# Sorted block attention and a residual MLP on one core: SyncE in program order, mixing of batches 2 and 3 moved to ScalarE one stage earlier, score and product groups in pairs

## The chip, the core and the metric

The kernel runs on one NeuronCore of one Trainium2 chip. The metric is the device time of one execution in microseconds (us), measured on that core. The engines are named as in the profile: PE is TensorE (matmuls; PEld is its weight load), DVE is VectorE, ACT is ScalarE, POOL is GpSimd and SP is SyncE, which here issues DMAs only. All engines run their own instruction streams and meet through semaphores.

## The reference

Four batches, eight heads, 768 rows, head dimension 64. A small matrix per head (8 x 8) is normalised five times by rows and columns. Keys and values are mixed block by block with it (blocks of 96 rows), attention runs inside each block, and the result goes through a residual MLP: a product over tokens, then two channel products with a ReLU between.

```python
k_sorted = np.einsum('bhij,bhjcd->bhicd', P, k_b)      # mixing of 8 blocks of 96 rows
v_sorted = np.einsum('bhij,bhjcd->bhicd', P, v_b)
scores = scale * q_b @ k_sb.transpose(...)             # inside a block
attn = softmax(scores);  x = attn @ v_sb               # -> (B, S, 512)
tok = np.einsum('ts,bsd->btd', w_tok, alpha1 * x + beta1)
u = x + lam * tok
ch = np.maximum((alpha2 * u + beta2) @ w_ch1, 0.0) @ w_ch2   # 512 -> 2048 -> 512
out = u + lam * ch
```

## The kernel before

Work is written out by hand in one global order. After an opening that handles batch 0's attention, a main loop goes over eight steps: batch `b` (0 to 3) by half `hf` (0 and 1, 384 rows each). This text calls a step (b, hf). Each step has two parts:

- "h 0" to "h 15": one unit of the first channel product each (`h_unit`: four matmuls of 128x384 on PE, then a ReLU on ACT from `h_ps` to `hTa` or `hTb`);
- "c 0" to "c 11": a quarter of one of three row tiles of the second channel product each (`ch_unit`: four matmuls of 128x512). After c 3, c 7 and c 11 a tile is complete: DVE multiplies it by lambda (`ost`), POOL adds `u`, SP stores it (two DMAs).

All other work is hung into this raster with `put(b, hf, kind, n, ...)` and runs right after unit `n` of that step. PE therefore executes channel matmuls with attention pieces of the next batch in between:

- `mix_v(b, n)` and `mix_k(b, n)` (n = 0 to 2) mix values and keys of batch b on PE into `mix_ps` and `kmix_ps`. An engine given as an argument copies the result out: `mix_v` one copy of 128x1024 into `mixed`, `mix_k` four copies of 64x512 into `kT`. `mix_matrix(b)` builds the small matrices for it (one matmul, six short DVE operations).
- `bounce_v(b)` writes `mixed` to DRAM (`vscr`), `back_v(b)` reads it back as `Vs` with tokens on partitions, in runs of 128 bytes.
- `load_kv(b)` loads `raw` (values, then keys) with POOL's DMAs, `load_q(b)` loads `qn` likewise (six DMAs); `q_cross(b, kt)` turns `qn` into `qT` with six transposing DMAs on SP. Batch 1 alone turns its queries on PE.
- `score(b, g, hf)` is eight matmuls into `sc_ps` and an exponential on ACT (`et`); `pv(b, g, hf)` is eight matmuls with `Vs` into `x_ps`, then on DVE a reciprocal and a multiplication (`x`), and, one call later, two operations for `a` (kept in the list `late`, run by `flush`).
- `tails` copies row remainders of `a` and `x`; `moe_tok` is six matmuls of the token product (`tok_ps`), two DVE operations (`toktmp`, `u16`) and a POOL add; `moe_cross` turns `u16` into `uT` with three transposing DMAs on SP; `moe_affine` makes `a2T` on DVE, the input of the h units.

Two PSUM pools serve this: `psA` has two slots (`sc_ps`, `x_ps`, `mix_ps`, `kmix_ps`, `repv_ps`), `psB` has four (`h_ps`, `ch_ps`, `tok_ps`). Slots go round, so a matmul group waits until the reader of the tile that held its slot is done.

The order on PE, DVE, ACT and POOL is the written one: the wrapper class `Engine` calls `tc.keep_in_program_order`. SP is used without the wrapper before the change, so the scheduling layer places its DMAs. Before, for batch b = 2 and 3, mixing lies in step (b-1, 0) from h 8 on, `q_cross` at h 11 there (but the scheduler places the six transposes of batch 2 on SP ahead of the first store of step (0, 1)), scores and products from c 8 of step (b-1, 0) to h 11 of step (b-1, 1), and the loads for batch b+1 at c 11 of step (b-1, 0).

Of the kernel before, what the change touches and what calls it, by code (L numbers as in the profile page):

```python
# [16 lines left out]
def kernel(  # L17
# [20 lines left out]
    nc = tc.nc  # L38

    B, H, S, D = q.shape  # L40
    NB = sort_net.shape[-1]
    BLK = S // NB
    C = H * D
    HID = moe_w_ch1.shape[1]
    NT = S // 128
# [4 lines left out]
    H4 = H // 2  # L50
# [23 lines left out]
    dve = Engine(nc.vector)  # L74
    act = Engine(nc.scalar)
    pool = Engine(nc.gpsimd)

    dram = ctx.enter_context(tc.tile_pool(name="dram", bufs=1, space=bass.MemoryType.DRAM))
    wts = ctx.enter_context(tc.tile_pool(name="wts", bufs=1))
# [380 lines left out]
    def pv(b, g, hf):  # L460
        if g == 0 and hf == 0:
            x_of[b] = moep.tile([128, 8, C], F16, name="x128", tag="x128", bufs=2)
            a1_of[b] = moep.tile([128, 8, C], F16, name="a1", tag="a1", bufs=1)
        ps = psa([128, 2, 512], FT, "x_ps")[:].rearrange("p a (k d) -> p a k d", d=128)
        et = ets[(b, g, hf)][:].rearrange("p a i t -> p (a i t)")
        for ii in range(4):
            for h2 in range(2):
                lo = (4 * h2 + ii) * BLK
                w = min(128, 8 * BLK - lo)
                pe.matmul(  # L470
                    ps[0:w, h2, ii, 0:D + 1], et[0:BLK, lo:lo + w],
                    Vs[b % 2][0:BLK, (2 * g + h2) * NB + 4 * hf + ii, 0:D + 1], start=True, stop=True,
                )
        rc = att.tile([128, 2, 4], FT, name="rcb", tag="rc", bufs=3)
        dve.reciprocal(rc[0:BLK], ps[0:BLK, :, :, D])
        dve.tensor_tensor(
            x_of[b][0:BLK, 4 * hf:4 * hf + 4, g * 128:(g + 1) * 128].rearrange("p k (a d) -> p k a d", a=2),
            ps[0:BLK, :, :, 0:D].rearrange("p a k d -> p k a d"),
            rc[0:BLK].rearrange("p a k -> p k a").unsqueeze(3).to_broadcast([BLK, 4, 2, D]), ALU.mult,
        )  # L480
        flush()
        late.append(lambda: first_affine(b, slice(0, BLK), slice(4 * hf, 4 * hf + 4), slice(g * 128, (g + 1) * 128)))

    late = []

    def flush():
        while late:
            late.pop()()

    def tails(x, lo, hi, eng):  # L490
        flush()
# [3 lines left out]
    def q_cross(b, kt):  # L495
        if kt == 0:
            qT_of[b] = att.tile([128, H4, S], F16, name="qT", tag="qT", bufs=1)
        nc.sync.dma_start_transpose(
            qT_of[b][:, :, kt * 128:(kt + 1) * 128], qn_of[b][:, kt, :, :].rearrange("p h d -> p (h d)"),
        )  # L500

    def q_turn_late(b, g, eng):
        if g == 0:
            qT_of[b] = att.tile([128, H4, S], F16, name="qT", tag="qT", bufs=1)
        ps = psb([128, S], F16, "qt_ps")
        for kt in range(NT):
            pe.transpose(
                ps[:, kt * 128:(kt + 1) * 128],
                qn_of[b][:, kt, 2 * g:2 * g + 2, :].rearrange("p a d -> p (a d)"), ident16[:],
            )  # L510
        eng(qT_of[b][:, g, :], ps[:])
# [37 lines left out]

    def bounce_v(b):  # L550
        for th in range(2):
            nc.sync.dma_start(
                vscr[b, :, th * HB:(th + 1) * HB, :], mixed[b][th * 64:(th + 1) * 64, :, :],
            )

    def back_v(b):
        nc.sync.dma_start(Vs[b % 2][0:BLK, :, 0:D], vscr[b].rearrange("x t d -> t x d"))

    w_tokT = const([128, NT, S], F16, "w_tokT")
    wp_of = {}  # L560
# [106 lines left out]
    def moe_cross(b, hf):  # L667
        uT = uT_of[(b, hf)] = att.tile([128, CT, 384], F16, name="uT", tag="uT", bufs=2)
        for m in range(3):
            nc.sync.dma_start_transpose(  # L670
                uT[:, :, m * 128:(m + 1) * 128], u16_of[b][:, 3 * hf + m, :],
            )

    def moe_affine(b, hf):
        for ci in range(CT):
            affine(b, hf, ci, uT_of[(b, hf)][:, ci, :], dve)
# [25 lines left out]
    def last_out(hT, cps, kk, kt):  # L702
        for n in range(2):
            c = slice(n * C // 2, (n + 1) * C // 2)
            if n:
                cps = psb([128, C // 2], FT, "ch_ps")
                for m in range(HT):
                    pe.matmul(
                        cps[:], hT[m][:, kk * 128:(kk + 1) * 128], W2p[:, m, c],
                        start=(m == 0), stop=(m == HT - 1),  # L710
                    )
            ost = att.tile([128, C // 2], FT, name="ost", tag="ost", bufs=2)
            dve.tensor_tensor(ost[:], cps[:, 0:C // 2], lamB[:, c], ALU.mult)
            dve.tensor_tensor(ost[:], ost[:], u_of[B - 1][kt][:, c], ALU.add)
            nc.sync.dma_start(out[B - 1, kt * 96:(kt + 1) * 96, c], ost[0:96, :])
            nc.scalar.dma_start(out[B - 1, TAIL + kt * 32:TAIL + (kt + 1) * 32, c], ost[96:128, :])

    def ch_unit(b, hf, kk, part=(0, HT)):
# [19 lines left out]
        act_out(out[b, TAIL + kt * 32:TAIL + (kt + 1) * 32, :], ost[96:128, :])  # L738

    ch_of = {}  # L740
    act_out = nc.sync.dma_start

    copy = dve.tensor_copy

# [72 lines left out]
    def put(b, hf, kind, n, *todo):  # L817
        at.setdefault((b, hf, kind, n), []).extend(todo)
# [6 lines left out]
        put(0, 0, "h", 4 + kt, lambda kt=kt: moe_tok(0, kt, psb))  # L825
    for ks in range(NT):
        put(0, 0, "h", ks, lambda ks=ks: prep_wtok(ks, 1, psb, (dve.tensor_copy, act.copy)[ks % 2]))
    for n in range(1, B):
        put(max(n - 2, 0), n > 1, *(("h", 10), ("c", 9))[n > 1], lambda n=n: mix_matrix(n))
    put(0, 0, "h", 9, lambda: moe_cross(0, 1))  # L830
    for g in range(CT):
        put(0, 0, "h", g, lambda g=g: first_affine(0, slice(0, 128), slice(0, NT), slice(g * 128, (g + 1) * 128)))
    for m in range(3):
        put(0, 0, "h", 10 + m, lambda m=m: first_back(m, psb))
    put(0, 0, "c", 3, lambda: moe_affine(0, 1))
    for b in range(1, B):
        p = b - 1
        off = 3 if b == 1 else 0
        for n in range(3):
            put(p, 0, "h", (13 if b == 1 else 8) + n, lambda b=b, n=n: mix_v(b, n, dve.tensor_copy))  # L840
        put(p, 0, "h", 15 if b == 1 else 10, lambda b=b: bounce_v(b))
        put(p, 0, "c", 4 if b == 1 else 0, lambda b=b: back_v(b))
        for n in range(3):
            put(
                p, 0, *(("c", 3 + 3 * n) if b == 1 else (("h", 15), ("c", 1), ("c", 4))[n]),
                lambda b=b, n=n: mix_k(b, n, ((act.copy, dve.tensor_copy)[(n + (b > 1)) % 2],) * 4),
            )
        for kt in range(NT if b > 1 else 0):
            put(p, 0, "h", 11, lambda b=b, kt=kt: q_cross(b, kt))
        for g in range(0 if b > 1 else H4):  # L850
            put(p, 0, "c", off + (1, 4, 7, 7)[g], lambda b=b, g=g: q_turn_late(b, g, (dve.tensor_copy, act.copy, dve.tensor_copy, act.copy)[g]))
        if b + 1 < B:
            put(p, 0, "c", 11, lambda b=b: load_kv(b + 1), lambda b=b: load_q(b + 1))
        seq = [("s", 0), ("s", 1), ("s", 2), ("p", 0), ("s", 3), ("p", 1), ("p", 2), ("s", 4), ("p", 3), ("s", 5),
               ("p", 4), ("s", 6), ("p", 5), ("s", 7), ("p", 6), ("p", 7)]
        if b == 1:
            when = [("h", 0), ("h", 1), ("h", 2), ("h", 3), ("h", 4), ("h", 5), ("h", 6), ("h", 7), ("h", 8), ("h", 9),
                    ("h", 10), ("h", 11), ("h", 12), ("h", 13), ("h", 14), ("h", 15)]
        else:
            when = [("c", 8), ("c", 9), ("c", 10), ("c", 10), ("c", 11), ("c", 11), ("h", 0), ("h", 1), ("h", 2), ("h", 3),  # L860
                    ("h", 4), ("h", 5), ("h", 6), ("h", 8), ("h", 9), ("h", 11)]
        for (kind, n), (ph, at_) in zip(seq, when):
            f = (lambda b=b, n=n: score(b, n // 2, n % 2, psa)) if kind == "s" else (lambda b=b, n=n: pv(b, n // 2, n % 2))
            put(p, 1 if ph == "h" else 0, ph, at_, f)
        last = [("h", 12), ("h", 15)][b == 1]
        put(
            p, 1, *last, lambda b=b: tails(a1_of[b], 0, C, dve.tensor_copy),
            lambda b=b: tails(x_of[b], 0, C, dve.tensor_copy),
        )
        put(p, 1, "h", 4, lambda b=b: moe_start(b))  # L870
        for kt in range(3):
            put(p, 1, "c", 4 if b == 1 else 3, lambda b=b, kt=kt: moe_tok(b, kt, psb))
        put(p, 1, "c", 4 if b == 1 else 3, lambda b=b: moe_cross(b, 0))
        put(p, 1, "c", 8 if b == 1 else 7, lambda b=b: moe_affine(b, 0))
        for kt in range(3):
            put(b, 0, "h", 2 * kt, lambda b=b, kt=kt: moe_tok(b, 3 + kt, psb))
        put(b, 0, "h", 4, lambda b=b: moe_cross(b, 1))
        put(b, 0, "h", 13, lambda b=b: moe_affine(b, 1))

# [50 lines left out]
```

## Time and profile before

| what | value |
|---|---|
| time, median of 3 runs | 275.54 us (274.01 to 275.88) |
| time of the profiled execution | 275.76 us |
| span of the profiled execution, first to last instruction | 274.0 us |
| mean granted PE clock | 0.994 |
| PE busy | 260.2 us (95% of the span) |
| DVE, ACT, POOL busy | 169.7, 117.1, 96.4 us |
| DMA moved | 31.04 MB, POOL's queue 40.1% and SP's queue 30.9% of 16 engines' span |

The profile gives the busy time of each engine, groups of equal instructions with their mean duration, waits with what ended them, a timeline, and DMAs with the time from issue to landing. In rows such as `raw<-in_v_dram` the tile written stands left of the arrow. Nearly all rows carry the line L65, because the wrapper records every operation; one goes by tile names. L498, L552, L557, L670 and L737 are SP's own lines before the change (`q_cross`, `bounce_v`, `back_v`, `moe_cross`, the store). The steps of the main loop begin on PE at about 39.6 (0,0), 72.6 (0,1), 103.2 (1,0), 132.9 (1,1), 163.9 (2,0), 195.3 (2,1), 223.8 (3,0) and 248.4 us (3,1).

### The profile page before, as it was taken

The numbers are of one execution on the slowest core, as the hardware profiler recorded it, in microseconds if no ns is written. First come the engines' busy times: TensorE is split into PE (matmuls) and PEld (weight loads), VectorE is DVE, ScalarE is ACT, GpSimd is POOL, SyncE is SP. The second block draws the span as 40 slices with busy tenths as digits, with TensorE's granted clock in tenths as the row PEclk, the third lists the DMA queues.
The fourth block names the chain that finished last, engine by engine and source line by source line (L and its number), as shares of the span: only waits on it lengthen the run. The fifth ranks groups of instructions, "written<-read, shape, count | busy, mean of one in ns | idle before, by whom it ended". The sixth has DMA issues, their size and how long they took to land.

```text
span 274.0 us, 5366 instructions
## 1 busy us (share of the span) xinstructions
PE 260.2 (95%) x2159; PEld 140.4 (51%) x2173; DVE 169.7 (62%) x351; ACT 117.1 (43%) x219; POOL 96.4 (35%) x104
## 2 busy tenths in 40 slices
PE   7998899999999999999999969999999999999993
PEld 3466555455556444554455424564465445545552
DVE  5787527896468978576778725586689755121032
ACT  2588547234787002553674002554674004604600
POOL 8647102701472094403560824402200746122000
PEclk9999999999999999999999997999999999999999
DMA  6999999998989942249399952149300223012012
GB/s 103 211 206 193 206 207 214 173 115 178 128 176 175 133 116 78 59 115 145 86 182 165 113 138 61 38 118 117 106 10 2 76 58 77 22 38 77 0 41 77
DMA packets 67372, 31.04 MB, mean 113 GB/s; under 512 B 56642, under 2 KB 63058, under 8 KB 67348
## 3 DMA queue, kind: packets, MB, share of 16 engines
q0 software_dynamic: 26352, 15.34, 40.1%
q1 hardware_dynamic: 40900, 15.30, 30.9%
q8 instruction: 17, 0.28, 0.4%
q14 instruction: 7, 0.06, 0.1%
q10 hardware_dynamic: 96, 0.07, 0.1%
HBM read 32.79 MB, written 8.65 MB: 151 GB/s over the span
## 4 chain that ended last, share of the span: by engine, by line
PE 77%; DVE 9%; DMA 6%; issue 3%; SPq 2%; ACT 2%; POOL 0%; DVEq 0%; POOLq 0%
PE h_ps L65 30%; PE ch_ps L65 21%; PE tok_ps L65 10%; PE x_ps L65 3%; DMA out_dram<-ost 2%; PE sc_ps L65 2%; DVE ost L65 2%; DVE a L65 2%; DVE x L65 2%; PE warm_ps L65 2%; DMA q<-in_q_dram 2%; DMA uT<-u 2%; PE mix_ps L65 1%; PE kmix_ps L65 1%; SPq L737 1%
## 5 line engine op out<-in xcount | busy, mean ns | idle before, releaser
L65 PE MATMUL h_ps<-a2T,W1p 128*128 128x384 bf16 x512 | 97.2, 328 | 2.4 <-DVE a2T L65 2.1
L65 ACT ACTIVATE hTa<-h_ps 128x384 bf16<-128x384 f32 x96 | 47.0, 492 | 95.3 <-PE h_ps L65 95.1
L65 PE MATMUL ch_ps<-W2p,hTa 128*128 128x512 bf16 (+1 forms) x287 | 67.3, 370 | 0.6
L65 POOL TENSOR_TENSOR ost<-ost,u 128x512 f32<-128x512 f32 x21 | 26.6, 1267 | 116.1 <-DVE ost L65 110.0
L65 PEld LDWEIGHTS <-W1p 128*128 128x128 bf16 x512 | 47.6, 99 | 35.3 <-issue 5.0
L65 PEld LDWEIGHTS <-hTa 128*128 128x128 bf16 x300 | 28.4, 98 | 29.0
L65 DVE TENSOR_TENSOR ost<-ch_ps,lamB 128x512 f32<-128x512 f32 (+1 forms) x25 | 16.7, 670 | 37.9 <-PE ch_ps L65 34.6
L65 POOL TENSOR_TENSOR u<-toktmp,x 128x512 f32<-128x512 f32 x18 | 29.2, 1635 | 6.7 <-DVE toktmp L65 6.6
L65 PE MATMUL tok_ps<-a,w_tokT 128*128 128x512 f16 x126 | 30.5, 386 | 0.0
L65 ACT ACTIVATE et<-sc_ps 96x768 f16<-96x768 f32 (+1 forms) x32 | 25.6, 812 | 10.8 <-PE sc_ps L65 10.8
L65 PE MATMUL ch_ps<-W2p,hTb 128*128 128x512 bf16 (+1 forms) x99 | 24.8, 370 | 0.1
L65 DVE TENSOR_TENSOR toktmp<-tok_ps,lamB 128x512 f32<-128x512 f32 x21 | 14.4, 687 | 11.8 <-PE tok_ps L65 10.5
L65 PEld LDWEIGHTS <-w_tokT 128*128 128x128 f16 x126 | 12.3, 99 | 14.5 <-issue 1.1
L65 DVE TENSOR_TENSOR u<-toktmp,x 128x512 f16<-128x512 f32 (+1 forms) x24 | 18.9, 800 | 0.7
L65 ACT ACTIVATE hTb<-h_ps 128x384 bf16<-128x384 f32 x32 | 15.7, 490 | 8.0 <-PE h_ps L65 7.6
L65 POOL DMA_DIRECT2D qn<-in_q_dram x18 | 16.0, 924 | 4.7 <-DMA raw<-in_v_dram 4.7
L65 DVE CAST kT<-kmix_ps 64x512 f16<-64x512 f32 x20 | 14.2, 712 | 4.5 <-PE kmix_ps L65 3.0
L65 DVE TENSOR_TENSOR x<-x_ps,rcb 96x512 f16<-96x512 f32 x24 | 16.5, 686 | 0.8
L65 PE MATMUL x_ps<-Vs,et 96*128 96x65 f16 (+4 forms) x288 | 14.4, 195 | 2.3 <-DVE x L65 1.1
L65 DVE TENSOR_SCALAR a2T<-uT,ab2col 128x384 bf16<-128x384 f16 x28 | 10.6, 440 | 9.3 <-DMA uT<-u 9.3
L65 PEld LDWEIGHTS <-et 96*128 96x128 f16 (+4 forms) x288 | 12.4, 100 | 7.2 <-DVE x L65 2.3
L65 ACT CAST kT<-kmix_ps 64x512 f16<-64x512 f32 x16 | 11.5, 716 | 9.8 <-PE kmix_ps L65 9.6
(113 smaller groups left out, 237.8 us busy)
## 6 DMA issues: line engine op xcount, KB each, us to landing
out_dram<-ost SPq DMA_DIRECT2D x23, 192.0 KB, 2.4
raw<-in_v_dram POOLq DMA_DIRECT2D x6, 384.0 KB, 8.1
raw<-in_k_dram POOLq DMA_DIRECT2D x6, 384.0 KB, 10.0
qn<-in_q_dram POOLq DMA_DIRECT2D x18, 128.0 KB, 10.3
vscr<-mixed SPq DMA_DIRECT2D x6, 384.0 KB, 3.6
Vs<-vscr SPq DMA_DIRECT2D x3, 768.0 KB, 8.0
W1p<-in_moe_w_ch_dram POOLq DMA_DIRECT2D x4, 512.0 KB, 13.0
W2p<-in_moe_w_ch_dram POOLq DMA_DIRECT2D x4, 512.0 KB, 17.3
```

What stands on the lines that cost most here:

```text
L65: ins = getattr(self.eng, name)(*args, **kwargs)
L737: act_out(out[b, kt * 96:(kt + 1) * 96, :], ost[0:96, :])
```

## The change

1. SP goes through the wrapper (in `q_cross`, `bounce_v`, `back_v`, `moe_cross` and the stores), so its DMAs keep the written order.
2. The mixing of batches 2 and 3 moves from step (b-1, 0) to the c part of step (b-2, 1), and all its copies (`mixed` and `kT`) go to ACT. `bounce_v` and `q_cross` move with it; `mix_matrix(2)` and `mix_matrix(3)` move earlier too. `back_v(b)` and the loads of batch b+1 stand at h 6 of step (b-1, 0).
3. For batches 2 and 3 scores and products come two at a time, spread from h 15 of step (b-1, 0) to h 4 of step (b-1, 1), and `flush` is called at set places, first in first out.
4. For batches 2 and 3 the three `moe_tok` of the first half stand at c 0, c 1 and c 2 (all at c 3 before), `moe_cross` at c 2, `moe_affine` at c 6 (c 7 before), `tails` at h 8 (h 12 before).

The core of the diff:

```diff
+    sp = Engine(nc.sync)
...
-        flush()
+        if b == 1:
+            flush()
...
-            late.pop()()
+            late.pop(0)()
...
-        nc.sync.dma_start_transpose(
+        sp.dma_start_transpose(
...
+    put(0, 0, "h", 10, lambda: mix_matrix(1))
+    put(0, 0, "c", 6, lambda: mix_matrix(2))
+    put(1, 0, "h", 12, lambda: mix_matrix(3))
...
+    pairs = [("s", 0), ("s", 2), ("p", 0), ("s", 4), ("p", 2), ("s", 6), ("p", 4), ("p", 6)]
...
+            for n in range(3):
+                put(p - 1, 1, "c", 4 + n, lambda b=b, n=n: mix_v(b, n, act.copy))
+                put(p - 1, 1, "c", 7 + 2 * n, lambda b=b, n=n: mix_k(b, n, (act.copy,) * 4))
+            put(p - 1, 1, "c", 7, lambda b=b: bounce_v(b))
+            put(p, 0, "h", 6, lambda b=b: back_v(b))
+            for kt in range(NT):
+                put(p - 1, 1, "c", 6 + kt, lambda b=b, kt=kt: q_cross(b, kt))
+            if b + 1 < B:
+                put(p, 0, "h", 6, lambda b=b: load_kv(b + 1), lambda b=b: load_q(b + 1))
+            for (kind, n), at_ in zip(
+                pairs, ((0, "h", 15), (0, "c", 1), (0, "c", 3), (0, "c", 6), (0, "c", 8), (0, "c", 11), (1, "h", 1), (1, "h", 4)),
+            ):
+                if kind == "p":
+                    put(p, at_[0], at_[1], at_[2] + 1, flush)
+                for i in range(2):
+                    f = (lambda b=b, n=n + i: score(b, n // 2, n % 2, psa)) if kind == "s" else (lambda b=b, n=n + i: pv(b, n // 2, n % 2))
+                    put(p, *at_, f)
...
-            put(p, 1, "c", 4 if b == 1 else 3, lambda b=b, kt=kt: moe_tok(b, kt, psb))
-        put(p, 1, "c", 4 if b == 1 else 3, lambda b=b: moe_cross(b, 0))
-        put(p, 1, "c", 8 if b == 1 else 7, lambda b=b: moe_affine(b, 0))
+            put(p, 1, "c", 4 if b == 1 else kt, lambda b=b, kt=kt: moe_tok(b, kt, psb))
+        put(p, 1, "c", 4 if b == 1 else 2, lambda b=b: moe_cross(b, 0))
+        put(p, 1, "c", 8 if b == 1 else 6, lambda b=b: moe_affine(b, 0))
```

Here p is b - 1. Batch 1's places stay as they were, and PE executes the same matmuls in all.

More of the change, by code (lines that the diff above doesn't have):

```diff
@@ L551, in bounce_v @@
         for th in range(2):
-            nc.sync.dma_start(
+            sp.dma_start(
                 vscr[b, :, th * HB:(th + 1) * HB, :], mixed[b][th * 64:(th + 1) * 64, :, :],
@@ L556, in back_v @@
     def back_v(b):
-        nc.sync.dma_start(Vs[b % 2][0:BLK, :, 0:D], vscr[b].rearrange("x t d -> t x d"))
+        sp.dma_start(Vs[b % 2][0:BLK, :, 0:D], vscr[b].rearrange("x t d -> t x d"))
     w_tokT = const([128, NT, S], F16, "w_tokT")
@@ L669, in moe_cross @@
         for m in range(3):
-            nc.sync.dma_start_transpose(
+            sp.dma_start_transpose(
                 uT[:, :, m * 128:(m + 1) * 128], u16_of[b][:, 3 * hf + m, :],
@@ L714, in last_out @@
             dve.tensor_tensor(ost[:], ost[:], u_of[B - 1][kt][:, c], ALU.add)
-            nc.sync.dma_start(out[B - 1, kt * 96:(kt + 1) * 96, c], ost[0:96, :])
+            sp.dma_start(out[B - 1, kt * 96:(kt + 1) * 96, c], ost[0:96, :])
             nc.scalar.dma_start(out[B - 1, TAIL + kt * 32:TAIL + (kt + 1) * 32, c], ost[96:128, :])
@@ L740 @@
     ch_of = {}
-    act_out = nc.sync.dma_start
+    act_out = sp.dma_start
     copy = dve.tensor_copy
@@ L827 @@
         put(0, 0, "h", ks, lambda ks=ks: prep_wtok(ks, 1, psb, (dve.tensor_copy, act.copy)[ks % 2]))
-    for n in range(1, B):
-        put(max(n - 2, 0), n > 1, *(("h", 10), ("c", 9))[n > 1], lambda n=n: mix_matrix(n))
+    put(0, 0, "h", 10, lambda: mix_matrix(1))
+    put(0, 0, "c", 6, lambda: mix_matrix(2))
+    put(1, 0, "h", 12, lambda: mix_matrix(3))
     put(0, 0, "h", 9, lambda: moe_cross(0, 1))
@@ L835 @@
     put(0, 0, "c", 3, lambda: moe_affine(0, 1))
+    pairs = [("s", 0), ("s", 2), ("p", 0), ("s", 4), ("p", 2), ("s", 6), ("p", 4), ("p", 6)]
     for b in range(1, B):
         p = b - 1
[L838 to L855, printed above, removed]
@@ L856 @@
-        if b == 1:
-            when = [("h", 0), ("h", 1), ("h", 2), ("h", 3), ("h", 4), ("h", 5), ("h", 6), ("h", 7), ("h", 8), ("h", 9),
-                    ("h", 10), ("h", 11), ("h", 12), ("h", 13), ("h", 14), ("h", 15)]
-        else:
[L860 to L864, printed above, removed]
@@ L865 @@
-        last = [("h", 12), ("h", 15)][b == 1]
+        if b == 1:
+            for n in range(3):
+                put(0, 0, "h", 13 + n, lambda n=n: mix_v(1, n, dve.tensor_copy))
+                put(0, 0, "c", 3 + 3 * n, lambda n=n: mix_k(1, n, ((act.copy, dve.tensor_copy)[n % 2],) * 4))
+            put(0, 0, "h", 15, lambda: bounce_v(1))
+            put(0, 0, "c", 4, lambda: back_v(1))
+            for g in range(H4):
+                put(0, 0, "c", (4, 7, 10, 10)[g], lambda g=g: q_turn_late(1, g, (dve.tensor_copy, act.copy)[g % 2]))
+            put(0, 0, "c", 11, lambda: load_kv(2), lambda: load_q(2))
+            seq = [("s", 0), ("s", 1), ("s", 2), ("p", 0), ("s", 3), ("p", 1), ("p", 2), ("s", 4), ("p", 3), ("s", 5),
+                   ("p", 4), ("s", 6), ("p", 5), ("s", 7), ("p", 6), ("p", 7)]
+            for at_, (kind, n) in enumerate(seq):
+                put(0, 1, "h", at_, (lambda n=n: score(1, n // 2, n % 2, psa)) if kind == "s" else (lambda n=n: pv(1, n // 2, n % 2)))
+        else:
+            for n in range(3):
+                put(p - 1, 1, "c", 4 + n, lambda b=b, n=n: mix_v(b, n, act.copy))
[14 more added lines that the diff above has]
+                    put(p, *at_, f)
@@ L866 @@
         put(
-            p, 1, *last, lambda b=b: tails(a1_of[b], 0, C, dve.tensor_copy),
+            p, 1, "h", 15 if b == 1 else 8, lambda b=b: tails(a1_of[b], 0, C, dve.tensor_copy),
             lambda b=b: tails(x_of[b], 0, C, dve.tensor_copy),
```

## The prediction

> **What bounds the kernel now.** I read the page's busy line first, then PE's waits, the timeline and stage windows around the longest of them, SP's waits, and last the DMA issues.
>
> ```profile
> PE 260.2 (95%) x2159; PEld 140.4 (51%) x2173; DVE 169.7 (62%) x351; ACT 117.1 (43%) x219; POOL 96.4 (35%) x104
> PE h_ps L65 <- DVE a2T L65: 2.1, 1, 2.1
> PE x_ps L65 <- DVE x L65: 1.1, 2, 0.6
> SPq L498 <- DMA qn<-in_q_dram: 25.6, 2, 13.3
> ```
>
> PE is busy for 95% of the span and its matmuls are the same after the change, so only its gaps and its slow stretches can move. The largest lies between steps (1,1) and (2,0):
>
> ```profile
> 159.98 1.04 PE L65 MATMUL ch_ps<-W2p,hTa 128*128 128x512 bf16 x4
> 160.85 1.03 PE L65 MATMUL ch_ps<-W2p,hTb 128*128 128x512 bf16 x4
> 163.93 1.19 PE L65 MATMUL h_ps<-a2T,W1p 128*128 128x384 bf16 x4 [2.05 <-DVE a2T L65]
> 164.97 2.27 PE L65 MATMUL tok_ps<-a,w_tokT 128*128 128x512 f16 x6
> 167.03 2.38 PE L65 MATMUL h_ps<-a2T,W1p 128*128 128x384 bf16 x8
> 166.00:167.00 1.00, 1.00 (x3) 0.30 (x2) 0.59 (x1) 0.00 (x0) 0.27 (x1) 0.50 0.00 0
> 148.86 8.20 SPq L498 DMA_TRANSPOSE qT<-qn  x6
> 158.25 4.13 SPq L670 DMA_TRANSPOSE uT<-u  x3
> ```
>
> PE idles for 2.05 us, then runs slowly: the window of 166 to 167 has a granted clock of 0.50. The cause is in the last two rows: SP spent 148.86 to 157.06 on six `qT` transposes that waited for `qn`, so `uT` came late, hence `a2T`, hence the first h unit.
>
> For what the change adds, the rows of ACT's copies, and of the transfers that will meet:
>
> ```profile
> L65 ACT CAST kT<-kmix_ps 64x512 f16<-64x512 f32 x16 | 11.5, 716 | 9.8 <-PE kmix_ps L65 9.6
> raw<-in_k_dram POOLq DMA_DIRECT2D x2, 384.0 KB, 11.1
> qn<-in_q_dram POOLq DMA_DIRECT2D x6, 128.0 KB, 11.9
> Vs<-vscr SPq DMA_DIRECT2D x1, 768.0 KB, 8.0
> q0 software_dynamic: 109, 0.57, 84.3%
> q1 hardware_dynamic: 48, 0.07, 5.2%
> ```
>
> The last two rows are the DMA view of 137 to 141: a store that SP issued at 135.09 is still moving its last 0.07 MB while POOL's loads of `raw` run, though a store of that size lands in 2.0 us on a free queue (196 to 216).
>
> **What the Trainium skill says.** "PSUM — Partial Sum Buffer", section "Engine vs sequencer instructions", has ScalarE's queue strictly first in, first out; the trace agrees, no ACT row overtakes another. "TensorE: Matmul & The Clock Gate", section "What's actually happening", has the clock halve after an idle window of about 3.4 us and return after a busy one; the trace shows 0.50, but after 2.05 us of idling with a half-idle first unit behind it. "TensorEngine Tiling (Array Packing)", section "Key Properties", says that a change of tiling mode drains the array; each score group (64 rows) here starts 0.10 us after the group before it ends. "DMA: Bandwidth & Descriptors", section "Queues, rings and completion order", has each DMA engine alternate between queues packet by packet, with about 9 to 17 descriptors in a typical packet; the late store agrees in direction, no view gives the packet's size.
>
> **The change part by part.**
>
> *Removed.* (a) `q_cross` now stands behind `moe_cross` on SP and `moe_tok` at c 0 to c 2: `uT` is issued some 5 us before h 0 of (2,0) needs it. The 2.05 us stall goes, and the slow clock: six `tok_ps` matmuls took 2.11 instead of 1.29, eight `h_ps` 2.17 instead of 1.30 (chain of waits), 1.69 together. (b) At (1,0) and (2,0) the first h unit was drawn out by `a2T` (1.03 to the next group instead of 0.65: twice 0.38), with a gap of 0.25 ahead of the first. In the changed order three mixing groups of 0.43 and three of 0.45 come before h 0 of (1,0), so it would start near 105.3; `a2T` is done near 104.1. Together 1.0. (c) `x_ps` waits for `x`, 1.1: in pairs, DVE's two reciprocals and multiplications (2 x 0.89) are done before PE comes back to the slot two c units later. (d) 16 score groups become 8 pairs: 8 x 0.10 = 0.8. Sum removed 2.05 + 1.69 + 1.0 + 1.1 + 0.8 = 6.7 us. What is late next is below.
>
> *ACT.* I count from the start of `mix_v(b,0)` after c 4. PE's mixing groups start at 0, 1.3, 2.6 (values, one c unit of 0.87 between) and 3.9, 6.05, 8.25 (keys); h 0 runs 8.7 to 9.35, then `tok_ps`, h 1, h 2, until 11.95. A copy of 1024 on ACT does not occur before; from 0.492 for 384 and 0.807 for 768 elements it is about 1.05. So `mixed` is done at 4.3; twelve `kT` copies at 0.716 to 0.73 follow, four per group, starting at 4.6: done at 13.3. The ReLU of h 0 queues behind them and ends at 13.8. The second `tok_ps` needs h 0's slot (`psB` goes round by four: the third tile's store, h 0, `tok_ps`, h 1, h 2, and again), which PE wanted at 11.95. PE waits 1.9 us, at (1,0) and again at (2,0): 3.8. Bounds: 2.8 if the copies overlap a little, 4.4 if the long copy is as slow as DVE's 1.218; and the clock may fall after each (0 or 1.7 more, by the stretch above); I take 3.8 and no fall, since a wait of 1.9 between dense stretches is a little less idling than the one before. `mix_matrix(2)` at c 6 of (0,0) lets `kmix_ps` wait for ACT's copy of the first group: about 0.15. DVE's six operations there (1.4 us) lie beside ch matmuls.
>
> *Reading back `Vs`.* Place of time: end of the third `tok_ps` of (1,0), about 114.35 with the wait above. On SP `back_v(2)` stands behind the third `uT` transpose, whose `u16` comes 1.4 later and which takes 1.2: issue at 117.1. Before, that transfer landed 8.0 after issue: 125.1. PE needs it for the first pair of products at c 3: eleven h units (7.15), one `repv_ps` (0.13), two pairs of scores (2 x 0.67), four c units (3.46), so at 126.4. Spare 1.3 us. But `load_kv(3)` and `load_q(3)` stand beside it: POOL reaches them after its third add (the add starts 0.9 after `tok_ps` ends and takes 1.66), at 116.9, with the first bytes 1.5 later, 118.4; the first bytes of `Vs` come at 118.1, since the DMA engines began 1.0 after its issue before. They meet almost entirely. `raw` needs about 10.1 us of the DMA engines (136.2 to the landing of the keys at about 146.8, less the receipt) and `qn` about 7.7 (145.0 to 152.7; the DMA view of 145 to 152 holds 6211 packets of its queue). If `Vs` went first it would land in time: lower bound 0. If every small run waited for one of the large ones and then shared with `qn`, it would be last: 10.1 + 7.7 = 17.8 late, 16.5 after the spare time. Per DMA engine `Vs` has 6144 / 16 = 384 runs and `raw` 256 / 16 = 16: with 16 runs a turn (the skill's typical packet) all of `raw` passes first, 10.1; with 32 a turn 12 of 16 pieces, 7.6. Small and large pieces overlap somewhat (DMA share 1.6 in the windows with small runs, 1.0 with `raw` alone), so I take 8.3 late, a PE stall of 7.0. All later work stands behind it on PE; nothing gives it back. An idle stretch of this length drops the clock: 1.7 more. For batch 3 no load follows, so `Vs` lands 1.3 before its products.
>
> The stores behind `Vs` on SP are late too; two `ost` buffers and the stall itself cover that. Exponentials in pairs (2 x 0.81) finish within the two c units (1.73) before the next scores. `a` is complete with `tails` at h 8 some 2 us before c 0. These cost nothing.
>
> *Sum:* -6.7 + 3.8 + 0.15 + 7.0 + 1.7 = +5.95 on the profiled execution's 275.76, so 281.7; the median of the runs is 0.22 below it: 281.5.
>
> **The rivals.** *B, `Vs` arrives in time.* Same waits, no stall at c 3, because SP's first runs enter 0.3 us ahead and the queues share kindly. -6.7 + 3.95 = -2.75: 272.8. For it: 1.3 us of spare time and a slow start of `raw`. Against it: the delayed store. It decides at 1.3 us of delay; up to 4.0 us of delay, without a clock drop, the result stays not slower. *C, ACT does not hold PE either:* if the copies run ahead enough, -6.7 + 0.15: 269.0. Against it: 11.8 us of copies between 0.6 and the ReLU, one in-order engine. *D, the gains fail:* SP's written order makes `uT` wait for a store that waits for POOL; then 2.05 and 1.69 stay and time is some 3.7 above A, 285.2. In (1,1) the first store follows c 3 but `uT` stands at c 2, so this is weak.
>
> **How the numbers follow.** A 0.57, B 0.28, C 0.11, D 0.04. A's own range is 275 (a stall of 2, partial removal of the clock drop) to 289 (a stall of 13, one clock drop by ACT). About 1% can be told from no change on this kernel, 2.76 us. A: 0.11 within, 0.46 slower; B: 0.14 faster, 0.12 within, 0.02 slower (a clock drop at ACT's waits); C: faster; D: slower. Faster 0.25, same 0.23, slower 0.52. The range 271 to 288 leaves out about 0.10 below and 0.08 above.
>
> **What would show it.** Right: a PE wait `x_ps` (its weight load) for `Vs<-vscr` of several us near 126, with the landing of that transfer well over 8.0 and the clock at 0.50 after it; two waits of `tok_ps` for ACT near 2 us at (1,0) and (2,0); no wait of `h_ps` for `a2T`; score rows in pairs. Wrong: `Vs` landing in about 8 us while `raw` moves, or ACT's ReLU of h 0 not late.

## The result, and the profile after

The changed kernel takes 287.63 us (median of 4 runs, 287.18 to 288.35), the kernel before 274.77 us beside it (273.17 to 275.88). The ratio is 1.0475 (95% interval 1.0411 to 1.0539): slower by 4.1 to 5.4%. The prediction said 281.5 us, slower, in a range of 271 to 288; the measured time lies at the upper edge of that range. The direction and the two waits it named were right; one of them was sized at little more than half of what it is.

The busy line of the kernel after:

```profile
PE 258.5 (90%) x2157; PEld 141.5 (50%) x2173; DVE 148.5 (52%) x329; ACT 134.6 (47%) x241; POOL 96.9 (34%) x104
```

Its longest PE waits (us in total, times, longest):

```profile
PE x_ps L65 <- DMA Vs<-vscr: 13.5, 2, 12.7
PE tok_ps L65 <- ACT hTa L65: 3.5, 2, 1.8
```

PE does the same matmuls in a longer span (busy for 90% of it instead of 95%). The waits of `h_ps` for `a2T` (2.1) and of `x_ps` for `x` (1.1) are gone from the list; two others stand there. PE's timeline shows both, and what follows the long one (start, us, operation, idle time before it):

```profile
106.86 1.46 PE L65 MATMUL tok_ps<-a,w_tokT 128*128 128x512 f16 x6
108.16 1.46 PE L65 MATMUL h_ps<-a2T,W1p 128*128 128x384 bf16 x8
111.39 1.46 PE L65 MATMUL tok_ps<-a,w_tokT 128*128 128x512 f16 x6 [1.77 <-ACT hTa L65]
...
126.36 1.03 PE L65 MATMUL ch_ps<-W2p,hTb 128*128 128x512 bf16 x4
140.04 1.09 PE L65 MATMUL x_ps<-Vs,et 96*128 96x65 f16 x16 [12.65 <-DMA Vs<-vscr]
140.94 1.47 PE L65 MATMUL ch_ps<-W2p,hTa 128*128 128x512 bf16 x3
142.63 2.45 PE L65 MATMUL ch_ps<-W2p,hTa 128*128 128x512 bf16 x8 [0.22 <-issue]
```

Windows of one microsecond of the same kernel (length, PE busy, granted clock, DMA share, GB/s):

```profile
112.00:113.00 1.00, 1.00 (x6) 1.00 0.45 91
...
142.00:143.00 1.00, 0.78 (x2) 0.50 0.00 0
144.00:145.00 1.00, 1.00 (x6) 1.00 0.00 0
```

The second `tok_ps` waits 1.77 us for ACT and the clock stays whole behind it (1.00 at 112). At c 3 of (1,0) PE then stands for 12.65 us, and until about 143.8 it works at half the clock.

The timelines of ACT (first two rows), SP and POOL give the reasons:

```profile
102.12 8.70 ACT L65 CAST kT<-kmix_ps 64x512 f16<-64x512 f32 x12 [0.35 <-POOL u L65]
110.85 1.25 ACT L65 ACTIVATE hTa<-h_ps 128x384 bf16<-128x384 f32 x3
106.23 6.86 SPq L65 DMA_TRANSPOSE qT<-qn  x4
115.57 3.84 SPq L65 DMA_TRANSPOSE uT<-u  x3
119.47 1.05 SPq L65 DMA_DIRECT2D Vs<-vscr  x1
117.92 1.10 POOL L65 DMA_DIRECT2D raw<-in_v_dram  x2
119.01 1.05 POOL L65 DMA_DIRECT2D raw<-in_k_dram  x2
120.02 4.50 POOL L65 DMA_DIRECT2D qn<-in_q_dram  x5
```

Twelve key copies stand on ACT ahead of the ReLU of h 0. And `Vs` is issued 1.5 us after the first of POOL's loads. The DMA view tells what that does. First its issues in 119 to 141 (KB, us from issue to landing), then its queues in 125 to 128 and in 130 to 138 (packets, MB, share of 16 engines); `q0` is POOL's queue, `q1` SP's:

```profile
raw<-in_k_dram POOLq DMA_DIRECT2D x2, 384.0 KB, 9.5
Vs<-vscr SPq DMA_DIRECT2D x1, 768.0 KB, 20.4
qn<-in_q_dram POOLq DMA_DIRECT2D x6, 128.0 KB, 13.3
...
q0 software_dynamic: 118, 0.60, 97.1%
q1 hardware_dynamic: 118, 0.01, 5.8%
...
q0 software_dynamic: 4551, 0.57, 108.9%
q1 hardware_dynamic: 4553, 0.58, 91.7%
```

`Vs` lands after 20.4 us instead of 8.0. In both windows the two queues are served the same number of packets: 118 to 118 while POOL's are the 6144-byte pieces of `raw` (98 of them, the rest are 4-byte packets), 4551 to 4553 while they are the 128-byte runs of `qn`. One run of `Vs` for one piece of `raw` is next to nothing: 0.01 MB in 3 us. A shorter window shows the turn itself. A recorded piece of `raw` takes 0.473 us; in 125.55 to 126.01, which is about one piece long, each queue has 16 packets, as many as there are DMA engines:

```profile
q0 software_dynamic: 16, 0.10, 102.8%
q1 hardware_dynamic: 16, 0.00, 5.7%
```

One more thing stands in these packets. The first run of `Vs` starts at 124.9, 5.4 us after the issue; in the run with the loads moved (loads_later, below) it is 1.2 us. Until then SP's queue carries `uT`, issued ahead of `Vs` on the same queue and slowed by the same loads: 512 packets of 256 bytes from 122.2 on.

### The profile page after: what moved, and what is told of

It is laid out like the page before. It is cut to its first block, busy times and chain, and to the rows that moved or that the text cites. A ratio compares the mean times of both kernels' runs of the same rounds, so it can differ in the third digit from the quotient of the medians.

```text
span 285.8 us, 5358 instructions
## 1 busy us (share of the span) xinstructions
PE 258.5 (90%) x2157; PEld 141.5 (50%) x2173; DVE 148.5 (52%) x329; ACT 134.6 (47%) x241; POOL 96.9 (34%) x104
## 4 chain that ended last, share of the span: by engine, by line
PE 74%; DMA 11%; ACT 7%; DVE 3%; issue 2%; SPq 2%; DVEq 0%
PE ch_ps L65 23%; PE h_ps L65 23%; PE tok_ps L65 10%; DMA Vs<-vscr 10%; ACT kT L65 6%; PE warm_ps L65 4%; PE x_ps L65 4%; PE sc_ps L65 2%; SPq L65 2%; PE mix_ps L65 1%; PE v_ps L65 1%; DVE ost L65 1%; PE turn_ps L65 1%; PE wtok_ps L65 1%; PE q_ps L65 1%
## 5 line engine op out<-in xcount | busy, mean ns | idle before, releaser
L65 PE MATMUL h_ps<-a2T,W1p 128*128 128x384 bf16 x512 | 92.0, 326 | 0.3 <-ACT a2T L65 0.3
L65 ACT ACTIVATE hTa<-h_ps 128x384 bf16<-128x384 f32 x96 | 46.4, 493 | 53.3 <-PE h_ps L65 53.0
L65 PE MATMUL ch_ps<-W2p,hTa 128*128 128x512 bf16 (+1 forms) x287 | 69.3, 375 | 0.9 <-issue 0.2
L65 PEld LDWEIGHTS <-W1p 128*128 128x128 bf16 x512 | 48.2, 98 | 31.8 <-issue 0.2
L65 ACT ACTIVATE et<-sc_ps 96x768 f16<-96x768 f32 (+1 forms) x32 | 24.9, 811 | 32.6 <-PE sc_ps L65 32.6
L65 PE MATMUL x_ps<-Vs,et 96*128 96x65 f16 (+4 forms) x288 | 13.5, 198 | 14.1 <-DMA Vs<-vscr 13.5
L65 ACT CAST kT<-kmix_ps 64x512 f16<-64x512 f32 x32 | 22.9, 715 | 6.3 <-PE kmix_ps L65 5.6
L65 PEld LDWEIGHTS <-w_tokT 128*128 128x128 f16 x126 | 12.2, 98 | 17.8 <-issue 4.1
L65 DVE TENSOR_SCALAR a2T<-uT,ab2col 128x384 bf16<-128x384 f16 x28 | 9.9, 418 | 15.5 <-DMA uT<-u 11.3
L65 DVE TENSOR_TENSOR u<-toktmp,x 128x512 f16<-128x512 f32 (+1 forms) x24 | 17.4, 735 | 0.7
L65 DVE RECIPROCAL rcb<-x_ps 96x8 f32<-96x8 f32 x24 | 4.8, 199 | 20.7 <-PE x_ps L65 20.6
## 6 DMA issues: line engine op xcount, KB each, us to landing
Vs<-vscr SPq DMA_DIRECT2D x3, 768.0 KB, 20.4
```

What stands on the lines that cost most here:

```text
L65: ins = getattr(self.eng, name)(*args, **kwargs)
```

## The experiments

All edits below are made to the changed kernel unless the text says otherwise; times are medians, ratios are to the kernel before, measured beside each.

**The loads at c 4 (loads_later).**

```diff
-                put(p, 0, "h", 6, lambda b=b: load_kv(b + 1), lambda b=b: load_q(b + 1))
+                put(p, 0, "c", 4, lambda b=b: load_kv(b + 1), lambda b=b: load_q(b + 1))
```

> Only edit to the changed kernel: both loads of the batch after next (keys, values, queries) are issued at c 4 of the same step instead of h 6. Theory A (the Vs read-back is slow because it shares the DMA engines with these loads): Vs lands 8 to 9 us after issue instead of 20.4, PE's wait at c 3 falls from 12.65 to 0 to 1.5 us, the slow clock behind it (about 1.8) goes: 287.6 - 12 to 14.4 = 273 to 276 us. Rival B (Vs is late by itself, because of SP's order or its small pieces): landing stays near 20, time stays above 284.

Measured: 272.7 us, ratio 0.9936 (0.9917 to 0.9955), a little under the 273 to 276 of theory A. Its DMA view of 119 to 129 and its waits:

```profile
Vs<-vscr SPq DMA_DIRECT2D x1, 768.0 KB, 8.0
PE tok_ps L65 <- ACT hTa L65: 3.5, 2, 1.8
PE x_ps L65 <- DMA Vs<-vscr: 0.7, 1, 0.7
```

`Vs` is issued at 118.84, almost as late as in the changed kernel, and lands in 8.0. So the meeting with the loads makes the 12.65 us, and SP's order without the loads does not. From the start of the `x_ps` group at c 3 to the next `sc_ps` group PE takes 3.19 us here (126.97 to 130.16) and 4.97 in the changed kernel (140.04 to 145.01): the slow clock, with a gap of 0.22 us in it, cost 1.8 us.

**Which of the loads.** Only the queries at c 4 (queries_later), or only keys and values (keys_values_later):

```diff
-                put(p, 0, "h", 6, lambda b=b: load_kv(b + 1), lambda b=b: load_q(b + 1))
+                put(p, 0, "h", 6, lambda b=b: load_kv(b + 1))    # keys_values_later: load_q here,
+                put(p, 0, "c", 4, lambda b=b: load_q(b + 1))     # and load_kv here
```

> Only the load of the queries moves from h 6 to c 4; keys and values stay at h 6. If the raw loads hold Vs back in full (they pass first, as the prediction took for its 10.1), Vs lands near 119.2 + 9.4 + 6.3 = 135, PE waits about 7.7 us, time about 282. If all three share evenly the raw loads cost Vs only what it loses by sharing: landing 130 to 133, wait 3 to 6, time 277 to 281. If only the queries matter, no wait and about 274.

> The counterpart: only keys and values move from h 6 to c 4; the queries stay at h 6. If the raw loads are what holds Vs back, Vs lands near 8 to 10 us after issue, wait 0 to 2, time 273 to 277. If the small pieces of the queries share with those of Vs, landing is up to 14 us after issue (6.3 + 7.7), wait up to 6, time up to 281.

Measured: with the queries later 283.86 us (ratio 1.035, 1.029 to 1.0411), wait of PE 9.74; with keys and values later 279.69 us (1.0201, 1.0132 to 1.027), wait 5.05. The landings of `Vs`, in the same order:

```profile
Vs<-vscr SPq DMA_DIRECT2D x1, 768.0 KB, 17.5
Vs<-vscr SPq DMA_DIRECT2D x1, 768.0 KB, 12.7
```

The first falls on the first of its expectations ("pass first": 282), a little above it; the second on the case of shared small pieces. Either load alone is enough for a stall, and the two do not add up: 9.5 and 4.7 us late alone, 12.4 together. The packets say how. With `raw` alone 29, 39 and 75 runs of `Vs` start in the microseconds from 125 to 128, and 965 to 1045 in each from 129 to 134, when `raw` is through. With `qn` alone it is 565 to 572 of `Vs` and 557 to 566 of `qn` in each microsecond from 125 to 129. Serving one for one reproduces the end: in the changed kernel the last piece of `raw` starts at 128.6, and 6144 runs at 567 per us take 10.8, so 139.4; the last packet of `Vs` starts at 139.5.

**The backlog on ACT, alone (half_copies_dve).** The second of the three groups of key copies goes to DVE, four copies of twelve (a third, though the run's name says half):

```diff
-                put(p - 1, 1, "c", 7 + 2 * n, lambda b=b, n=n: mix_k(b, n, (act.copy,) * 4))
+                put(p - 1, 1, "c", 7 + 2 * n, lambda b=b, n=n: mix_k(b, n, ((act.copy, dve.tensor_copy)[n % 2],) * 4))
```

> Only edit: the four key copies of the second group (c 9) of batches 2 and 3 go to DVE instead of ACT. Theory A (ACT's backlog of copies holds the ReLU of h 0 and with it the slot that tok_ps needs): both PE waits of tok_ps for ACT (1.75 each) go, 287.6 - 3.5 = 284.1. Rival: the wait only moves to another slot or DVE's tail delays u16 and so uT; then 287 to 288.

Measured: 288.89 us, ratio 1.0532 (1.0471 to 1.0592). The expectation of 284.1 was a miss, though the ACT waits did go:

```profile
PE x_ps L65 <- DMA Vs<-vscr: 17.0, 2, 14.7
PE tok_ps L65 <- ACT hTa L65: 0.5, 2, 0.3
```

PE comes to the products of c 3 2.0 us earlier (140.07 - 14.71 = 125.36 against 140.04 - 12.65 = 127.39) and waits 2.06 us longer, to the same moment. At batch 3, where no load stands beside the transfer, the wait for `Vs` grows from 0.84 to 2.24. What PE gains ahead of a transfer that it does not set is handed back at that transfer. SP's row is why it does not set it: `Vs` is issued at 119.99 here, behind transposes, though the three tiles of `u16` are done at 114.9 instead of 117.0. The loads add to it: they start earlier too, `uT` moves beside them until 129.0, and the first run of `Vs` starts only at 129.1. The slow clock also lasts longer: the eight `ch_ps` matmuls behind the wait take 3.43 us instead of 2.45.

**The read-back ahead of the `uT` transposes (back_earlier),** loads left at h 6:

```diff
-            put(p, 0, "h", 6, lambda b=b: back_v(b))
+            put(p, 0, "h", 1, lambda b=b: back_v(b))
```

> Only edit to the changed kernel: the read-back of Vs is issued at h 1 instead of h 6, so it stands on SP ahead of the three uT transposes; the loads stay at h 6. Theory A (collision): Vs is issued near 115 instead of 119.5, moves from about 116 to 122, of which only the last 3 us meet raw (first packets at 119.2); landing 8 to 12 us after issue, no wait of PE at c 3, time 273 to 276 (the two ACT waits of 1.75 stay). Rival B (a read-back on this queue takes 20 us wherever loads are under way): landing at 135, wait about 8, time 282.

Measured: 281.78 us, ratio 1.0273 (1.0217 to 1.033). The landing was as theory A had it (issued at 115.24, landing 7.8) and the time was not. SP, DVE and PE:

```profile
115.24 0.57 SPq L65 DMA_DIRECT2D Vs<-vscr  x1
115.91 12.37 SPq L65 DMA_TRANSPOSE uT<-u  x3
135.68 1.25 DVE L65 TENSOR_SCALAR a2T<-uT,ab2col 128x384 bf16<-128x384 f16 x4 [13.79 <-DMA uT<-u]
138.42 0.50 PE L65 MATMUL sc_ps<-qT,kT 64*128 64x96 f16 x8 [8.17 <-DVE x L65]
```

Now `uT` stands behind `Vs` on SP: its packets wait for those of `Vs` until 122.0 and then meet the loads. `moe_affine` at h 13 waits for it on DVE for 13.79 us, the multiplications of the products queue behind it, and PE waits 8.17 us for their slot. The meeting has found another victim, and its way to PE leads through DVE's order.

**SP in program order, and nothing else (before_sp_order),** in the kernel before:

```diff
+    sp = Engine(nc.sync)
...
-        nc.sync.dma_start_transpose(
+        sp.dma_start_transpose(
...
-    act_out = nc.sync.dma_start
+    act_out = sp.dma_start
```

> The kernel before with one part of the change alone: SyncE's DMA issues kept in the program's order, nothing moved. The prediction's term (a): uT of (2,0) no longer stands behind six qT transposes that wait for qn, so the 2.05 us stall and 1.69 of slow clock go: 274.5 - 3.7 = 270.8. Rival: the qT transposes now stand ahead of the read-back of Vs at h 11 and 15, it is issued near 126, lands near 134 and the products at c 10 wait for it, 1 to 3 us at each of batches 2 and 3: 273 to 276.

Measured: 285.68 us, ratio 1.0403 (1.0347 to 1.046). Its waits:

```profile
PE x_ps L65 <- DMA Vs<-vscr: 8.8, 2, 5.2
PE sc_ps L65 <- DMA qT<-qn: 2.6, 2, 1.5
```

Both the expected gain and the rival are there. The time on PE from c 0 of (1,1) to h 0 of (2,0) falls from 16.69 (147.24 to 163.93) to 14.48 (153.97 to 168.45), the next h part from 18.09 to 16.02: 4.3 us, of which the prediction's term (a) has 3.7 and half of (b) 0.5. But six `qT` transposes now stand ahead of `Vs` (issued at 127.90 and 194.71), and the c parts of (1,0) and (2,0) grow from 13.30 each to 19.98 and 21.26. The rival was under-priced: 2.6 and 8.8 us of waits, and the slow clock behind them. So the wrapper alone does not pay here; in the change, which moves `q_cross` as well, no wait for `qT` is left. The move without the wrapper was not run.

**Three edits together (all_three):** loads at c 4, the second group of key copies on DVE, `back_v` at h 1, as in the diffs above. Then the same with scores and products one by one (singles), in the order of the kernel before (the list `seq`, left out here):

```diff
...
+            when = [("c", 0), ("c", 1), ("c", 2), ("c", 3), ("c", 4), ("c", 5), ("c", 6), ("c", 7), ("c", 8), ("c", 9),
+                    ("c", 10), ("c", 11), ("h", 0), ("h", 1), ("h", 3), ("h", 5)]
+            for (kind, n), (ph, at_) in zip(seq, when):
...
+                put(p, 1 if ph == "h" else 0, ph, at_, f)
```

> The changed kernel with three edits: loads at c 4, key copies of the second group on DVE, read-back of Vs at h 1. The loads at c 4 alone gave 272.7 with two ACT waits of 1.75 and one Vs wait of 0.7 left. If the waits are independent once Vs is early enough, these 4.2 us go: 268.5. If the copies on DVE alone only move the wait (as they did with the loads at h 6, where Vs was late), 271 to 273.

> The kernel with the three edits, and scores and products of batches 2 and 3 one by one again, one group after each of the c units 0 to 11 and h units 0, 1, 3, 5, instead of pairs. The prediction's terms (c) and (d) say that pairs save 1.1 us of waits of products for x and 0.8 of gaps (8 groups by 0.10): 268.5 + 1.9 = 270.4. Rival: the pairing is worth nothing, since with one group per c unit DVE's 0.89 fits between two groups: 268.5.

Measured: 271.56 us (ratio 0.9911, 0.9871 to 0.9951) and 272.39 us (0.993, 0.9904 to 0.9957). The three edits gained less than the 268.5 expected for independent waits. The number falls into the second case of the expectation (271 to 273), but not for its reason: the waits for ACT did go (0.5 us left), and PE waits for `x` in their place. DVE and PE of the first:

```profile
126.59 1.25 DVE L65 TENSOR_SCALAR a2T<-uT,ab2col 128x384 bf16<-128x384 f16 x4 [6.43 <-DMA uT<-u]
129.32 0.34 PE L65 MATMUL sc_ps<-qT,kT 64*128 64x96 f16 x8 [0.82 <-DVE x L65]
```

`uT` behind `Vs` on SP is late for h 13 again, by less since no load is beside it. The two times don't settle what pairs are worth, because their intervals overlap. The traces do for the groups: from h 0 of (1,0) to c 0 of (1,1), less the waits for DVE in it, PE takes 40.24 us in pairs (41.55 - 1.31) and 41.21 one by one (41.44 - 0.23), 0.97 for 16 groups against 8.

**`moe_affine` at c 6 (affine_later)** of the same step, on top of the three edits; then the same with one of them undone, its diff above read backwards: `back_v` at h 6 (back_at_h6), the loads at h 6 (affine_later_loads_h6), all copies on ACT (copies_all_act).

```diff
-        put(b, 0, "h", 13, lambda b=b: moe_affine(b, 1))
+        put(b, 0, "c", 6, lambda b=b: moe_affine(b, 1))
```

> The kernel with the three edits, and moe_affine of the second half moved from h 13 to c 6, so that on DVE the products' reciprocals and multiplications no longer stand behind operations that wait for uT. The four PE waits of sc_ps for x (2.4 us in all) go: 271.6 - 2.4 = 269.2. Rival: the affine operations at c 6 are now late for the next half's first h unit or delay the second pair's x: 270.5 to 272.

> As affine_later, but the read-back of Vs at h 6 as in the change, behind the uT transposes. SP, not PE, sets its issue (118.8 to 120.0 in the runs so far), so with PE 1.5 earlier at c 3 (near 124.9) and a landing 8 us after issue PE waits 2 to 3 us at batch 2 and about 2 at batch 3: 269.2 + 4 to 5 = 273 to 274. Rival: Vs is issued earlier because the transposes of u16 are free earlier: 269 to 270.

> As affine_later, but the loads back at h 6, as in the change. Theory: the meeting of transfers costs only what stands behind the loser; here uT loses (landing near 134) and nothing of this step waits for it, only the next half's h 0, near 134.5 plus 1.7 of DVE's affine: 1 to 2 us more than affine_later, about 270.5 to 271. Rival: any meeting with the loads costs several us, as in the two runs with loads at h 6 before: 276 or more.

> As affine_later (loads at c 4, Vs at h 1, affine at c 6), but all key copies of batches 2 and 3 on ACT again, as in the change. With no late transfer to swallow it, ACT's backlog should cost what the prediction's term says in kind: two waits of tok_ps for ACT of 1.75 each less the 0.6 that is left with half of the copies on DVE, 268.4 + 2.9 = 271.3. Rival: the wait lets SP and the transfers run ahead and part of it comes back later: 268.5 to 270.

Measured for the first: 268.43 us, ratio 0.9777 (0.9726 to 0.9827), faster than both kernels and 0.8 below its expectation. Its busy line and longest waits:

```profile
PE 256.2 (96%) x2157; PEld 140.8 (53%) x2173; DVE 156.7 (59%) x337; ACT 128.9 (48%) x233; POOL 96.8 (36%) x104
PE warm_ps L65 <- DVE wz L65: 1.2, 1, 1.2
PE tok_ps L65 <- ACT hTa L65: 0.6, 2, 0.3
```

No wait of PE in the main loop is over 0.3 us. The other three, one step undone in each:

| undone | us | ratio to before | wait of PE that came back |
|---|---|---|---|
| `back_v`, to h 6 | 274.31 | 0.9965 (0.9935 to 0.9995) | `x_ps` for `Vs`, 1.70 and 2.28 |
| loads, to h 6 | 278.49 | 1.014 (1.0071 to 1.0209) | `x_ps` for `Vs`, 6.26 |
| second group of copies, to ACT | 271.42 | 0.9871 (0.9815 to 0.9928) | `tok_ps` for ACT, 3.5 in two |

The first and the last come within 0.3 us of their expectations (273 to 274, 271.3). With `back_v` at h 6 `Vs` is issued at 119.14, within 0.4 us of the changed kernel, though PE is ahead: SP sets it. The loads at h 6 were a miss on the theory's side: POOL, no longer held by the ACT wait, issues them at 115.62, their packets start at 118.55 when a little over half of `Vs` is through, and `Vs` loses instead of `uT`. The rival's 276 or more was right. A fixed place in the order is no fixed time on another queue.

## Why the prediction came out as it did

*Removed, -6.7* (its terms add up to 6.64). This was right in total. In the profiled executions the spans differ by 11.8 (285.8 - 274.0). The added waits and the slow clock make 3.5 + 13.5 + 1.8 = 18.8, so 7.0 was removed. This is a remainder, known to about 1 us: the start of step (0,1) is 73.37 in the changed kernel, 72.85 in loads_later and 72.38 in queries_later, though nothing before it differs between these three, and by the medians (12.9 apart) 5.9 was removed. The `a2T` stall and its slow clock are gone as term (a) said. Term (d) was counted short: it took the score groups of both batches and left out the products, which pair up as well; the run one by one shows 0.97 per batch, so about 1.9 instead of 0.8. That the total came out all the same is in part luck: others among (a) to (c) were too large by about as much, or the remainder hides it; which, the runs do not tell.

*ACT, +3.8.* This was right in size and in mechanism: the waits are 1.77 and 1.72, no clock drop stands behind them, and they cost 2.6 to 3.0 us of time where nothing hides them (ratios 0.9871 against 0.9777, medians 271.42 against 268.43, taken at different times). Alone the gain could not be seen, since `Vs` took it back.

*`Vs`, +7.0.* The mechanism, the place, the queue and the clock drop (1.7 predicted, 1.8 measured) were right; the size is 12.65. Three terms of the sum make the difference, and the first is the largest:

- The delay by the loads: 8.3 taken, 12.4 measured (20.4 - 8.0). The step that failed is the turn of a DMA engine between its queues. The prediction let 16 or 32 runs of `Vs` pass in each turn, the 16 after the section "Queues, rings and completion order" of "DMA: Bandwidth & Descriptors", whose typical packet has about 9 to 17 descriptors. In this trace the queues change after every recorded packet (16 to 16 in the time of one piece, 118 to 118, 4551 to 4553). The measurement decides: one run a turn. Then `Vs` passes behind all of `raw` and afterwards shares evenly with `qn`, which the 10.8 us above reproduce; in the 8.3 the sharing with `qn` had no part. The upper bound had the right turn, but its 17.8 put all of `qn` first as well, which was too much. The prediction also let the first bytes of `Vs` move 1.0 after the issue and overlooked `uT` ahead of it on the same queue (5.4). In the changed kernel this costs little by itself, since beside `raw` only 32 to 46 runs of `Vs` pass in a microsecond.
- The issue: 117.1 expected, 119.47 measured. The prediction had `back_v` wait for the third `u16`; it waits for SP. Four `qT` transposes take 6.86 us there, the store and one more follow, and the three `uT` issues start at 115.57 although the first two tiles were ready at 109.85 and 114.37. This is 2.4 us more. About 1.3 of it is SP (an estimate: the third tile was ready at 116.97, and one issue of 1.2 behind it would end near 118.2); the rest is PE and DVE coming later than predicted.
- The need: 126.4 expected, 127.39 measured (140.04 - 12.65), which gives 1.0 back. So 7.0 becomes 7.0 + 4.1 + 2.4 - 1.0 = 12.5, and 0.17 more lie between landing (139.87) and the matmul.

At batch 3, "`Vs` lands 1.3 before its products" failed by the same late SP: 0.84 of waiting.

*The rivals.* B needed a delay under 1.3 us. It is what happens when the loads are moved (272.7, predicted 272.8), so the working of its time was good and its cause absent. D (SP's written order makes the gain void) did not happen in the change; in the kernel before with the wrapper alone another written order, `qT` ahead of `Vs`, cost 4%. No run contradicts "All later work stands behind it on PE"; what the prediction did not see is that the loser of the meeting can be chosen: `Vs` in the change, `uT` with `back_v` ahead of it.

## What to carry to other kernels

Before placing a transfer of small runs beside one of large pieces, count runs and not bytes: in these traces each queue got one packet a turn, so the small one stood almost still until the large one was through. Sum up the issue time of everything ahead on the issuing queue (here, from 106 on, five transposes of `qT` and three of `uT` at 1.2 to 1.7 us each) before taking a data dependence for the start of a DMA. And when one wait is taken away and the time does not fall, look for the next thing that PE does not set: here the ACT wait was worth about 3 us once the read-back was early, and nothing before.

## What the runs showed of the hardware that was not expected

- Two queues that both had work were served packet for packet over 3 and over 8 us, at sizes of 128 against 6144 bytes and of 128 against 128.
- With nothing beside it `Vs` moves 958 to 1257 of its 128-byte runs per us over the 16 DMA engines (loads_later, 120 to 125), beside `qn` about 567, and beside `raw` 32 to 46 (changed kernel, 125 to 128).
- The time from POOL's issue to the first packets varied: 1.3 us for `raw` in the changed kernel (117.92 to 119.19), 2.9 with the loads at h 6 in the last set (115.62 to 118.55) and 3.9 with the read-back ahead (117.68 to 121.59), where they began just as `Vs` ended. In the last two `Vs` was already moving alone when POOL issued or soon after (first runs at 115.8 and 116.5), in the first it was not. Whether this is the reason is open; it decides which transfer loses.
- The length of a wait alone does not tell whether the clock falls. It stayed whole after waits of 1.77, 1.72 and 1.70 us, fell after 2.05 (the kernel before) and 2.28 (back_at_h6, where eight `ch_ps` matmuls behind it take 3.16 us), and stayed whole after 2.24 at batch 3 of half_copies_dve:

```profile
201.86 0.69 PE L65 MATMUL x_ps<-Vs,et 96*128 96x65 f16 x16 [2.24 <-DMA Vs<-vscr]
202.00:203.00 1.00, 1.00 (x19) 1.00 0.40 102
```

"TensorE: Matmul & The Clock Gate", section "What's actually happening", speaks of an idle window of about 3.4 us; in two of these runs a shorter gap was enough, in the others it was not, and what decides between 2.05 and 2.28 us is open here.
